# Cluster attention, experts and a bilinear layer: one engine for the low parts of the experts' weights

## The chip, the cores and the metric

One core of a Trainium2 chip runs the kernel. Its engines are TensorE (PE; PEld is its loading of weights), VectorE (DVE), ScalarE (ACT), GpSimd (POOL) and SyncE (SP), which issues most of the DMAs; GpSimd issues the indirect ones. Each works through its own queue in order and waits on semaphores for the others. The metric is the time on the device in microseconds.

## The reference

```python
# attention: 2 x 8 heads, 768 rows of 64; a query sees the keys of its own cluster of 16
q_assign = np.argmax(np.einsum('bhsd,hcd->bhsc', q_n, c_n), axis=-1)
k_assign = np.argmax(np.einsum('bhsd,hcd->bhsc', k_n, c_n), axis=-1)
mask = q_assign[:, :, :, None] == k_assign[:, :, None, :]
scores = np.where(mask, scale * np.matmul(q, k.transpose(0, 1, 3, 2)), -1000000000.0)
x = softmax(scores) @ v                       # then laid out as 1536 tokens x 512
# experts: 8, one to a token, 512 -> 1024 -> 512, times the gate
logits = x @ w_gate
expert_idx = np.argmax(logits, axis=1)
for e in range(E):
    h = np.maximum(x[expert_idx == e] @ w1[e], 0.0)
    out[expert_idx == e] = gate_w[expert_idx == e, None] * (h @ w2[e])
# bilinear layer: 512 -> 1536, weights in float64
return (out @ w_a) * (out @ w_b) @ w_out
```

## The kernel before

The kernel has three stages on the time line of the profile: attention to about 295 us, the experts to 520, the bilinear layer from 526 to the end. Every engine's order is the order in which the program writes its instructions; nothing is scheduled afterwards.

A float32 operand is multiplied as two float32r parts, a high part (`hi`, `xh`, `hh`) that a copy rounds, and a low part (`lo`, `xl`, `hl`) that a subtraction makes from the operand and its high part; a product takes three matmuls. The experts' weights come in pieces of 128 x 1024 elements, 512 KB each, eight to an expert: four of `w1`, then four of `w2`. `piece_load` issues a piece's DMA on SyncE into one of four buffers `raw`, `piece_parts` (lines 129 to 141) makes `hi` on ScalarE and `lo` on the engine that `ENG` names, by the piece's number modulo the length of that list: even pieces on GpSimd, odd ones on VectorE. The load of a piece is issued behind the parts of the piece four before it, and takes its buffer. Pieces 0 and 1 are split during the attention; 35 even and 35 odd ones of the experts follow.

The experts' stage works on windows of 256 tokens, one to an expert, in the order 0 to 3, a spill window of 128 rows (`spill`) for the largest expert, then 4 to 7. In a window (`window`, lines 959 to 988) eight groups of 12 matmuls make the blocks of the hidden layer into three banks in turn; ScalarE makes `hh`, VectorE `hl` from each, so the fourth group needs the bank that the first `hl` frees. Eight more groups make `y`. While they run, the next window's rows are transposed and split (`xh`, `xl`, line 957). At the end `store` copies `y` to `yt`, half on ScalarE, half on VectorE (lines 991, 992).

Side work is spread by `tick`, which each group calls once. It asks for pieces ahead of their use (at tick t up to number `t // 2 + min(LEAD + t // 4, 10)`), and takes one step of the generator `tables`: counts and offsets of the experts, the table of further windows, then `gates` (the softmax's value at the chosen expert, squared) and the places `pu` to which each token's number and gate are scattered (`aux`, by GpSimd; read back behind the loop for further windows, line 1201). `tables` gets a step in each of the first ticks, from tick 1 to 14, and after that in the second half of each window.

```python
    ENG = [("act", "pool"), ("act", "dve")]
    ENG64 = [("act", "pool")]
        if t >= 1 and (t < 15 or t % 16 >= 8):
            next(tab_steps, 0)
```

The weights of the bilinear layer (`ENG64`) are first put from float64 to float32 on VectorE, and their low parts are made by GpSimd.

Of the kernel before, what the change touches and what calls it, by code (L numbers as in the profile page):

```python
# [8 lines left out]
F32 = mybir.dt.float32  # L9
# [20 lines left out]
def cluster_attention__then__moe__then__bilinear_kernel(  # L30
# [37 lines left out]
    # ---- weights in chunks of [128, 1024], each split into two float32r parts  # L68
# [7 lines left out]
    # A piece is what one staging tile holds: a chunk of w1 (256 columns) or of  # L76
    # w2 (256 rows), or half a chunk of w_a, w_b or w_out, which come as float64
    # and are read as pairs of 32-bit words.
# [26 lines left out]
    def piece_bits(n):  # L105
        """First part of a split: float64 to float32."""
        t = raw_t.pop(n)
        i, j = pieces[n]
        if j == 0:
            s = i % NSLOT  # L110
            pn = pools["a" if s < NA else "b"]
            hi_t[i] = pn.tile([128, CH], F32R, tag=f"hi{s}", name=f"hi_{i}")
            lo_t[i] = pn.tile([128, CH], F32R, tag=f"lo{s}", name=f"lo_{i}")
        if i >= MOE2:
            # float64 to float32: sign and top exponent bit stay, the other three
            # bits by which the exponents differ go, the fraction is cut to 23 bits
            # (exact for zeros, and to 24 bits in float32's normal range)
            r = t.rearrange("p (f w) -> p f w", w=2)
            tmp = pools["b"].tile([128, CH // 2], U32, tag="tmp", name=f"tmp_{n}", bufs=2)
            nc.vector.tensor_scalar(out=tmp, in0=r[:, :, 1], scalar1=5, scalar2=2,  # L120
                                    op0=ALU.logical_shift_left, op1=ALU.logical_shift_right)
            nc.vector.scalar_tensor_tensor(out=tmp, in0=r[:, :, 1], scalar=0xC0000000, in1=tmp,  # L122
                                           op0=ALU.bitwise_and, op1=ALU.bitwise_or)
            nc.vector.scalar_tensor_tensor(out=tmp, in0=r[:, :, 0], scalar=29, in1=tmp,  # L124
                                           op0=ALU.logical_shift_right, op1=ALU.bitwise_or)
            t = tmp
        bits_t[n] = t.bitcast(F32)

    def piece_parts(n, hi_eng, lo_eng):
        """Second part of a split: high and low float32r."""  # L130
        raw = bits_t.pop(n)
        i, j = pieces[n]
        hi, lo = hi_t[i], lo_t[i]
        if i >= MOE2:
            hi, lo = (x[:, CH // 2 * j:CH // 2 * j + CH // 2] for x in (hi, lo))
        if hi_eng == "act":
            nc.scalar.copy(out=hi, in_=raw)  # L137
        else:
            nc.vector.tensor_copy(hi, raw)
        eng = nc.gpsimd if lo_eng == "pool" else nc.vector  # L140
        eng.tensor_tensor(out=lo, in0=raw, in1=hi.bitcast(F32), op=ALU.subtract)  # L141
# [5 lines left out]
    # ---- scratch in DRAM: a region of S*B rows for each expert  # L147
# [4 lines left out]
    # ---- constants of the routing  # L152
# [39 lines left out]
    # =========================== attention ===========================  # L192
    # Tiles that are free first come first: the first chunks of the experts' weights
    # take their place before the attention has ended.
# [9 lines left out]
    lg = {}  # L204
# [58 lines left out]
    # Operand stacks of 128 rows, two sets that take turns. First head of a pair:  # L263
    # queries [high; low] and [high; cluster], keys [high; high] and [low; penalty];
    # second head: the halves swapped. The cluster and penalty rows are 16 in 32.
# [8 lines left out]
    # centroids over their norms, laid out as a block diagonal for each head pair  # L274
# [31 lines left out]
    # The norm of a query or key row scales its similarities by one positive  # L306
    # factor, so it does not change which centroid has the largest one.
    class Prep:
        """The steps that lay out the operands of a pair of heads."""
# [17 lines left out]
        def sims(self, tag="X", bufs=1):  # L327
            # similarities, transposed: row 32 g + 16 h + c
            x = ps.tile([128, 512], F32, tag=tag, name=f"sm{self.p}", bufs=bufs)
            for g in range(4):  # L330
                nc.tensor.matmul(
                    x[32 * g:32 * g + 32, 0:GN], lhsT=cblk[:, self.hp, :],
                    rhs=self.raw["qk"[g // 2]][:, GN * (g % 2):GN * (g % 2) + GN], start=True, stop=True,
                )
            self.sim = ap.tile([128, GN], F32, tag="sim", name=f"sim{self.p}")
            nc.scalar.copy(out=self.sim, in_=x[:, 0:GN])
# [21 lines left out]
        def rows(self, nm, tag="X", bufs=1, copies=(act_copy, dve_copy, act_copy, dve_copy)):  # L358
            # cluster rows of the queries, penalty rows of the keys
# [21 lines left out]
        def high(self, nm, h, i, other, copy):  # L381
            """High parts: those of head h, in stack i, own half or (keys) the other one."""
            r = slice(64 * h, 64 * h + 64)
            o = slice(64 - 64 * h, 128 - 64 * h) if other else r
            dst = (qs if nm == "q" else ks)[self.s, h]
            copy(dst[o, i, :], self.raw[nm][r])
# [59 lines left out]
    def pv_steps(p, g, j0=0, nj=NG, tags=("O", "X"), per=1):  # L446
        """Values times probabilities for nj query tiles of a group, in steps."""
# [22 lines left out]
    def emit_x(p, t0, nj, ot, sm, tag):  # L470
        b, hp = pairs[p]
        if hp == 0 and t0 == 0:
            xb[b] = xpool.tile([128, NT, DM], F32, name=f"x{b}")
            lg[b] = xpool.tile([128, NT, E], F32, name=f"lg{b}")
# [21 lines left out]
    # =========================== routing ===========================  # L496
# [4 lines left out]
    def apart(group, inst, why):  # L501
        """Scatters of a group go to rows of their own: none waits for another."""
        inst = inst.ins
        tc.declare_no_dep(inst, group=group, reason=why)
        tc.add_to_no_dep_group(group, inst)
# [7 lines left out]
    def route(b, t0, n, tag="X", place=None):  # L513
        """Experts of n tiles of tokens and the rows of xs that they go to, in steps.
        With place, no scatter, but one-hot rows for the places in the first window."""
# [57 lines left out]
    def gates(b):  # L573
# [8 lines left out]
        nc.vector.tensor_scalar(out=g, in0=g, scalar1=1e-9, scalar2=None, op0=ALU.add)  # L582
        nc.vector.reciprocal(out=g, in_=g)
# [5 lines left out]
    def tables(rps):  # L589
        """Counts and offsets of the experts, positions of the tokens, windows  # L590
        beyond the first, in steps."""
# [15 lines left out]
        # the expert with the most tokens, and where its further window starts  # L607
# [21 lines left out]
        # all windows beyond the first, one to a partition  # L629
# [28 lines left out]
        # start of each window inside its expert, then the three columns of the table  # L658
# [16 lines left out]
        # where the tokens go: number and squared gate of each  # L675
        yield from gates(B - 1)
        dl = cp.tile([128, E], F32, name="dl")
        nc.vector.tensor_tensor(out=dl, in0=off, in1=erow, op=ALU.subtract)
        for b in range(B):
# [3 lines left out]
            nc.vector.tensor_reduce(out=ps_, in_=t, axis=AX.X, op=ALU.add)  # L683
            nc.vector.tensor_tensor(out=ps_, in0=ps_, in1=slot[b], op=ALU.add)
# [9 lines left out]
    # ---- the attention's schedule  # L694
    NU = 12
    LAG = 2
    def keep_warm(n, tag, shape, bufs, pool=ps):
        """The PE array's clock halves when it idles for a few microseconds."""
# [67 lines left out]
    for p in range(1, len(pairs)):  # L766
        for o, step in STEPS:
            if p == 1:
                # no values to multiply yet: the first four steps in two iterations
# [12 lines left out]
    def steps_at(i, gen, n=1, every=1):  # L782
        """The next n steps of gen, one in each of the coming iterations."""
# [13 lines left out]
    # The last group of the last pair goes one query tile after another. The tokens  # L797
    # of its last NP tiles come into the first window by products with one-hot rows,
    # the others by way of xs, where rows not yet written hold zeros.
# [11 lines left out]
    def place_split(t, c0, c1, copy):  # L811
        """Columns of tile t in two float32r parts."""
# [11 lines left out]
    def place_mm(t, d):  # L824
        """Adds the tokens of tile t to the transposed rows of the first window."""
# [75 lines left out]
    # =========================== experts ===========================  # L901
# [11 lines left out]
    def advance(n, engines, later=0):  # L913
        """Splits up to piece n, of the last ones only the first part, and loads."""
# [31 lines left out]
    def win_xt(w, n, a):  # L946
        """Transposes of the rows 128 a ... of a window, and their split."""
# [48 lines left out]
    def spill(w, c0, tick, nxt):  # L996
        """A window of 128 rows with the rows stationary; returns its last part."""
# [68 lines left out]
    ENG = [("act", "pool"), ("act", "dve")]  # L1066
# [29 lines left out]
    # the first banks are those that the first window's rows are read from until late  # L1096
# [56 lines left out]
    # ---- any further windows, one at a time  # L1153
# [42 lines left out]
    # =========================== bilinear layer ===========================  # L1196
# [28 lines left out]
    for gr in range(NGR):  # L1225
        for st in range(NST):
# [3 lines left out]
            for fl in range(GF + 1):  # L1230
# [24 lines left out]
                # of the very last tile of tokens, two blocks together at the end  # L1255
# [49 lines left out]
```

## Time and profile before

| | us |
|---|---|
| median of 3 timed runs | 832.33 |
| lowest and highest | 831.39, 832.38 |
| span of the profiled execution, first to last instruction | 830.4 |
| busy: PE, DVE, ACT, POOL | 793.5, 541.5, 367.1, 292.9 |

The profile gives the execution's own time as its span; what a timed run has beyond that is the little work around it. Busy time is added up over stages with different limits, so what a change in one stage is worth is read from the waits of that stage.

### The profile page before, as it was taken

How to read it: one execution, taken by the hardware profiler on the slowest of the kernel's cores; microseconds unless marked ns; L12 is line 12 of the kernel's file. 1: busy time of each engine (PE TensorE's matmuls, PEld its weight loads, DVE VectorE, ACT ScalarE, POOL GpSimd, SP SyncE). 2: the span in 40 equal slices, each digit the busy share in tenths (PEclk: the TensorE clock that was granted, in tenths of full speed). 3: DMA queues.
4: the chain of work that ended last, by engine and by line, in shares of the span. 5: the costliest groups of instructions: out<-in, count | busy, mean ns of one | idle time of the engine just before them, and what ended most of it. 6: DMA issues, size and time to landing. Idle time of an engine off the chain costs nothing. (4 is left out here: it accounts for less than half of the span.)

```text
span 830.4 us, 12569 instructions
## 1 busy us (share of the span) xinstructions
PE 793.5 (96%) x4832; PEld 639.1 (77%) x4832; DVE 541.5 (65%) x900; ACT 367.1 (44%) x693; POOL 292.9 (35%) x233
## 2 busy tenths in 40 slices
PE   8999999999999988899999999799999999999996
PEld 5666666665666778899999999588888888888885
DVE  6868879778786789555554459874565667624333
ACT  5867667766676454445564542222322212201100
POOL 4915434344540454576553334321121121101011
PEclk9999999999999999799999999899999999999998
DMA  9405012221100155768785654431131120001011
GB/s 299 97 1 159 1 39 63 64 58 45 52 20 1 50 197 167 225 148 221 230 276 184 218 183 153 117 114 51 51 93 60 51 70 32 1 0 51 1 51 51
DMA packets 69949, 81.91 MB, mean 99 GB/s; under 512 B 27264, under 2 KB 48256, under 8 KB 69888
## 3 DMA queue, kind: packets, MB, share of 16 engines
q1 hardware_dynamic: 67584, 74.78, 30.5%
q0 software_dynamic: 2304, 6.31, 2.0%
q8 instruction: 39, 0.64, 0.3%
q14 instruction: 22, 0.18, 0.1%
HBM read 70.58 MB, written 10.50 MB: 98 GB/s over the span
## 5 line engine op out<-in xcount | busy, mean ns | idle before, releaser
L141 POOL TENSOR_TENSOR lo<-raw,hi 128x1024 fp32r<-128x1024 f32 x37 | 92.7, 2509 | 88.8 <-ACT hi L137 43.6
L1242 PE MATMUL ab<-yh,hi 128*128 128x512 f32 x288 | 113.4, 394 | 6.0 <-ACT yh L1214 6.0
L141 POOL TENSOR_TENSOR lo<-tmp,hi 128x512 fp32r<-128x512 f32 x36 | 51.5, 1430 | 179.1 <-ACT hi L137 177.1
L1242 PE MATMUL ab<-yh,lo 128*128 128x512 f32 x288 | 113.1, 393 | 0.0
L1249 DVE TENSOR_TENSOR ga<-ga,ab 128x512 f32<-128x512 f32 x36 | 24.7, 685 | 127.3 <-PE ab L1242 104.4
L417 DVE TENSOR_REDUCE nm<-s 128x1 f32<-128x768 f32 x96 | 91.5, 953 | 17.9 <-PE s L415 12.4
L424 ACT ACTIVATE pr<-s,nm 128x768 f32<-128x768 f32 x96 | 87.2, 908 | 17.6 <-DVE nm L417 16.5
L438 PEld LDWEIGHTS t<-ident,pr 128*128 128x128 f32 x576 | 62.9, 140 | 40.6 <-ACT pr L424 16.8
L415 PE MATMUL s<-ks,qs 128*128 128x512 f32 (+1 forms) x384 | 91.2, 359 | 1.1 <-ACT pr L424 0.6
L438 PE MATMUL t<-ident,pr 128*128 128x128 f32 x576 | 83.8, 279 | 2.8 <-DVE pt L444 2.8
L1248 ACT COPY ga<-ab 128x512 f32<-128x512 f32 x36 | 21.1, 587 | 143.3 <-PE ab L1242 143.3
L453 PE MATMUL o<-pt,vn 128*64 128x384 f32 (+1 forms) x432 | 82.5, 472 | 0.0
L968 PE MATMUL h<-xh,hi 128*128 128x256 f32 x256 | 68.3, 297 | 10.2 <-DVE hl L973 10.0
L137 ACT CAST hi<-raw 128x1024 fp32r<-128x1024 f32 x70 | 72.4, 1047 | 12.6 <-DMA raw<-in_moe_w 12.5
L1242 PE MATMUL ab<-yl,hi 128*128 128x512 f32 x288 | 77.8, 392 | 0.0
L983 PE MATMUL y<-hh,hi 128*128 128x256 f32 x256 | 73.5, 287 | 0.0
L141 DVE TENSOR_TENSOR lo<-raw,hi 128x1024 fp32r<-128x1024 f32 x35 | 61.0, 1746 | 18.0 <-ACT hi L137 17.5
L983 PE MATMUL y<-hh,lo 128*128 128x256 f32 x256 | 72.4, 283 | 0.0
L983 PE MATMUL y<-hl,hi 128*128 128x256 f32 x256 | 72.4, 283 | 0.0
L442 ACT COPY pt<-t 128x384 f32<-128x384 f32 x98 | 46.9, 480 | 54.4 <-PE t L438 52.7
L1242 PEld LDWEIGHTS ab<-yh,hi 128*128 128x128 f32 x288 | 54.8, 190 | 17.6 <-ACT yh L1214 6.2
L415 PEld LDWEIGHTS s<-ks,qs 128*128 128x128 f32 x384 | 58.2, 189 | 12.1 <-issue 3.8
(309 smaller groups left out, 1682.3 us busy)
## 6 DMA issues: line engine op xcount, KB each, us to landing
raw<-in_moe_w SPq DMA_DIRECT2D x72, 512.0 KB, 4.6
raw<-in_moe_w_a SPq DMA_DIRECT2D x12, 512.0 KB, 3.7
raw<-in_moe_w_b SPq DMA_DIRECT2D x12, 512.0 KB, 3.7
raw<-in_moe_w_out SPq DMA_DIRECT2D x12, 512.0 KB, 3.3
xs<-zero SPq DMA_DIRECT2D x8, 512.0 KB, 5.2
xw<-xs SPq DMA_DIRECT2D x15, 256.0 KB, 5.5
vn<-in_v SPq DMA_DIRECT2D x8, 384.0 KB, 3.2
qn<-in_q SPq DMA_DIRECT2D x14, 192.0 KB, 4.8
```

The lines of the kernel that those rows point to most:

```text
L137: nc.scalar.copy(out=hi, in_=raw)
L141: eng.tensor_tensor(out=lo, in0=raw, in1=hi.bitcast(F32), op=ALU.subtract)
L415: nc.tensor.matmul(sc[:, c0:c1], lhsT=w, rhs=ks[s, h][:, i, c0:c1], start=(i == 0), stop=(i == 1))
L417: nc.vector.tensor_reduce(out=nm, in_=sc[:, 0:S], axis=AX.X, op=ALU.max, negate=True)
L424: nc.scalar.activation(out=pr, in_=sc[:, 0:S], func=AF.Exp, bias=nm, scale=1.0, accum_out=sums[p][:, t, h:h + 1])
L438: nc.tensor.transpose(x[:, 128 * n:128 * n + 128], pr[:, 128 * kb:128 * kb + 128], ident)
L442: nc.scalar.copy(out=dst, in_=src)
L453: nc.tensor.matmul(o[64 * h:64 * h + 64, 0:n], lhsT=vn[:, h, kb, :], rhs=pt_t[p, g, h][:, kb, 128 * j0:128 * j0 + n], start=(kb == 0), sto ...
L968: nc.tensor.matmul(hp_[:, 0:n], lhsT=a_[:, d, f0:f0 + 128], rhs=b_[:, d, 0:n], start=(i == 0), stop=(i == len(seq) - 1))
L983: nc.tensor.matmul(y[:, d, 0:n], lhsT=a_[:, fb % 2, 128 * d:128 * d + 128], rhs=b_[:, 0:n], start=(fb == 0 and d % 2 == 0 and i == 0), sto ...
L1242: nc.tensor.matmul(p_, lhsT=a_[:, d, f0:f0 + 128], rhs=b_[d], start=(i == 0), stop=(i == len(seq) - 1))
L1249: nc.vector.tensor_tensor(out=ga, in0=ga, in1=ab[1], op=ALU.mult)
```

## The change

All low parts of the experts' weights are made by VectorE. The logits `lg` are allocated in the pool of constants, which lives to the end, and not with the attention's output. The last batch's `gates` gets one step more, and in `tables` the places get steps of their own: one after `dl`, one after the first sum of each batch.

```diff
-            lg[b] = xpool.tile([128, NT, E], F32, name=f"lg{b}")
+            lg[b] = cp.tile([128, NT, E], F32, name=f"lg{b}")
...
-    def gates(b):
+    def gates(b, fine=False):
...
         nc.vector.tensor_scalar(out=g, in0=g, scalar1=1e-9, scalar2=None, op0=ALU.add)
+        if fine:
+            yield
         nc.vector.reciprocal(out=g, in_=g)
         nc.vector.tensor_tensor(out=auxt[b].bitcast(F32)[:, :, 1], in0=g, in1=g, op=ALU.mult)
         yield
...
-        yield from gates(B - 1)
+
+        yield from gates(B - 1, True)
         dl = cp.tile([128, E], F32, name="dl")
         nc.vector.tensor_tensor(out=dl, in0=off, in1=erow, op=ALU.subtract)
+        yield
         for b in range(B):
...
             nc.vector.tensor_reduce(out=ps_, in_=t, axis=AX.X, op=ALU.add)
+            yield
             nc.vector.tensor_tensor(out=ps_, in0=ps_, in1=slot[b], op=ALU.add)
...
-    ENG = [("act", "pool"), ("act", "dve")]
+    ENG = [("act", "dve")]
```

Comments are taken out too, and lines behind `gates` move down by up to four.

VectorE at the start of the experts' stage, from the last operation of the routing to the last of the first four low parts (the number behind a name is the buffer's; the lines' difference, before with -, after with +):

```order
 L560 TENSOR_TENSOR run_3347<-run_3299,ohe_143 128x8
-L1091 TENSOR_TENSOR xl_3395<-x0t_3301,xh_3394 128x512
-L1091 TENSOR_TENSOR xl_3395<-x0t_3302,xh_3394 128x512
+L141 TENSOR_TENSOR lo_3389<-raw_1068,hi_3388 128x1024
+L1095 TENSOR_TENSOR xl_3395<-x0t_3301,xh_3394 128x512
+L1095 TENSOR_TENSOR xl_3395<-x0t_3302,xh_3394 128x512
 L141 TENSOR_TENSOR lo_3401<-raw_1070,hi_3400 128x1024
+L141 TENSOR_TENSOR lo_3407<-raw_1366,hi_3406 128x1024
 L141 TENSOR_TENSOR lo_3413<-raw_1736,hi_3412 128x1024
```

Four low parts in place of two stand ahead of the first window's `hl`, the first of them ahead of the window's `xl`.

VectorE from the end of the gates to the second `hl` of the second window, before:

```order
L584 TENSOR_TENSOR auxt_84<-gg_3788 128x6
L141 TENSOR_TENSOR lo_3794<-raw_3654,hi_3793 128x1024
L678 TENSOR_TENSOR dl<-offs,erow 128x8
L681 TENSOR_TENSOR pt_3813<-ohe_142,dl 128x48
L683 TENSOR_REDUCE ps_3815<-pt_3813 128x6
L684 TENSOR_TENSOR ps_3815<-ps_3815,slot_144 128x6
L686 CAST pu_3818<-ps_3815 128x6
L992 ISA
L992 COPY yt<-y_3426 128x2x256
L973 SCALAR_TENSOR_TENSOR hl_0_3855<-h_0_3841,hh_0_3854 128x256
L141 TENSOR_TENSOR lo_3865<-raw_3751,hi_3864 128x1024
L973 SCALAR_TENSOR_TENSOR hl_1_3884<-h_1_3870,hh_1_3883 128x256
```

The same place now, from the sum of the gates on:

```order
L582 TENSOR_SCALAR gg_3788<-gg_3788 128x6
L141 TENSOR_TENSOR lo_3792<-raw_3654,hi_3791 128x1024
L585 RECIPROCAL gg_3788<-gg_3788 128x6
L586 TENSOR_TENSOR auxt_84<-gg_3788 128x6
L996 ISA
L996 COPY yt<-y_3426 128x2x256
L977 SCALAR_TENSOR_TENSOR hl_0_3843<-h_0_3829,hh_0_3842 128x256
L141 TENSOR_TENSOR lo_3847<-raw_3701,hi_3846 128x1024
L141 TENSOR_TENSOR lo_3853<-raw_3751,hi_3852 128x1024
L977 SCALAR_TENSOR_TENSOR hl_1_3872<-h_1_3858,hh_1_3871 128x256
```

The five operations from `dl` to `pu` have left the place ahead of the first `hl` (they follow in the window's second half), the last two of the gates stand behind the low part and not ahead of it, and a second low part stands ahead of the second `hl`. GpSimd's queue, which held 35 low parts between and behind its scatters there, holds the twelve scatters of `aux` alone until the bilinear layer's weights.

## Rows read from the trace of the kernel before

**Rows 1.** Busy time: length, PE, PEld, DVE, ACT, POOL, PEclk, DMA share, GB/s.

```profile
303.40:307.40 4.00, 4.00 (x21) 4.00 (x22) 3.72 (x14) 0.38 (x1) 2.17 (x1) 0.57 0.75 259
...
335.00:345.00 10.00, 9.21 (x43) 8.92 (x44) 5.71 (x7) 4.13 (x8) 5.56 (x2) 0.53 0.87 246
...
430.00:450.00 20.00, 20.00 (x170) 20.00 (x169) 9.41 (x13) 10.64 (x17) 7.76 (x4) 1.00 0.74 244
```

**Rows 2.** Timeline, TensorE's waits: start, length, instruction, [idle before <-releaser].

```profile
303.40 0.58 PE L968 MATMUL h<-xh,hi 128*128 128x256 f32 x1 [2.91 <-DVE hl L973]
...
327.78 0.74 PE L968 MATMUL h<-xl,hi 128*128 128x256 f32 x4 [2.09 <-DVE xl L957]
...
335.03 0.58 PE L968 MATMUL h<-xh,hi 128*128 128x256 f32 x1 [3.63 <-DVE hl L973]
...
338.72 0.58 PE L968 MATMUL h<-xh,hi 128*128 128x256 f32 x1 [0.76 <-DVE hl L973]
...
366.35 0.38 PE L968 MATMUL h<-xh,hi 128*128 128x256 f32 x1 [1.01 <-DVE hl L973]
...
415.13 0.50 PE L1032 MATMUL y<-hi,sl 128*128 128x512 f32 x1 [0.48 <-DVE sl L1023]
```

**Rows 3.** Timeline of VectorE, long rows of the experts' stage.

```profile
296.91 4.97 DVE L141 TENSOR_TENSOR lo<-raw,hi 128x1024 fp32r<-128x1024 f32 x1
...
304.00 1.60 DVE L604 CAST offi<-offs 128x8 int32<-128x8 f32 x1
...
310.99 2.00 DVE L639 TENSOR_TENSOR wcum<-wcum,wnw 128x1 f32<-128x1 f32 x1
...
315.76 2.04 DVE L639 TENSOR_TENSOR wcum<-wcum,wnw 128x1 f32<-128x1 f32 x1
...
318.21 2.21 DVE L645 TENSOR_TENSOR wn<-wn 128x1 f32<-128x1 f32 x1
...
323.35 2.17 DVE L666 TENSOR_TENSOR wst<-wva,ecol 128x80 f32<-128x80 f32 x1
...
362.43 3.54 DVE L141 TENSOR_TENSOR lo<-raw,hi 128x1024 fp32r<-128x1024 f32 x1 [0.51 <-ACT hi L137]
```

**Rows 4.** Timeline of GpSimd beside them.

```profile
296.02 4.76 POOL L141 TENSOR_TENSOR lo<-raw,hi 128x1024 fp32r<-128x1024 f32 x2
...
318.01 2.40 POOL L141 TENSOR_TENSOR lo<-raw,hi 128x1024 fp32r<-128x1024 f32 x1 [0.23 <-ACT hi L137]
```

**Rows 5.** Low parts by tile (min/median/max ns), and VectorE's group of the page.

```profile
L141 POOL TENSOR_TENSOR lo<-raw,hi x37: 2367/2406/3387, 119.3 to 487.2; 128x1024 fp32r<-128x1024 f32 x37
...
L141 DVE TENSOR_TENSOR lo<-raw,hi x35: 1209/1226/4967, 296.9 to 490.5; 128x1024 fp32r<-128x1024 f32 x35
...
L141 DVE TENSOR_TENSOR lo<-raw,hi 128x1024 fp32r<-128x1024 f32 x35 | 61.0, 1746 | 18.0 <-ACT hi L137 17.5
```

**Rows 6.** Timeline of VectorE, stage's start and second window's first `hl`.

```profile
295.48 1.29 DVE L1091 TENSOR_TENSOR xl<-x0t,xh 128x512 fp32r<-128x512 f32 x2 [2.16 <-ACT xh L1089]
...
332.50 0.16 DVE L678 TENSOR_TENSOR dl<-offs,erow 128x8 f32<-128x8 f32 x1
...
333.37 0.17 DVE L686 CAST pu<-ps 128x6 uint32<-128x6 f32 x1
...
334.56 0.41 DVE L973 SCALAR_TENSOR_TENSOR hl<-h,hh 128x256 fp32r<-128x256 f32 x1
```

**Rows 7.** Timeline of ScalarE, the gates' exponential and the next high part.

```profile
330.15 0.24 ACT L578 ACTIVATE gl<-gl 128x48 f32<-128x48 f32 x1 [7.21 <-DVE gl L577]
...
330.30 1.03 ACT L137 CAST hi<-raw 128x1024 fp32r<-128x1024 f32 x1
```

**Rows 8.** Timeline of GpSimd, scatters of places alone and beside a low part.

```profile
361.46 0.97 POOL L688 DMA_INDIRECT aux<-auxt,pu  x1 [0.30 <-issue]
...
365.04 1.80 POOL L688 DMA_INDIRECT aux<-auxt,pu  x1 [0.16 <-PE h L968]
```

**Rows 9.** Waits: who waited for whom, us in total, times, longest.

```profile
ACT hi L137 <- DMA raw<-in_moe_w: 12.5, 11, 1.9
```

## Prediction

> **What bounds the kernel now.** I read the table of stages first. In a window of the experts' stage that has got going, TensorE is busy all the time: 170 matmuls in 20.00 us at clock 1.00, so 0.118 us for one [rows 1]. There no change on another engine can give anything. What the change can give or take is therefore where TensorE waits in that stage, and for that I listed TensorE's waits from 300 to 420 us in order of time [rows 2]. The reader is to see what released each of them. All six end with a VectorE instruction: `hl` (the low part of a hidden block), `xl` (the low part of a window's rows) or `sl` (the same for the spill). They are 2.91, 2.09, 3.63, 0.76, 1.01 and 0.48 us. After two of the six the clock falls to its lower level: a granted clock of 0.57 over 4 us is 4 x 0.43 / 0.5 = 3.4 us at 1.2 GHz, and 0.53 over 10 us is 9.4 us of it [rows 1]. Each such microsecond costs half of itself.
>
> Next, why VectorE is late there. Seven of its rows are far too long for what they do [rows 3]: an addition of one element per partition takes 2.00 and 2.04 us. Put beside GpSimd's rows [rows 4] they end together: 318.21 + 2.21 = 320.42 against GpSimd's 318.01 + 2.40 = 320.41. The low part at 296.91 ends at 301.88, which is 1.10 us after GpSimd's two ended at 300.78: it did its own work only then. So a VectorE instruction between operands in SBUF stands still until GpSimd's low part is through. The table by tile says the same: VectorE's low parts have a median of 1.226 us and a maximum of 4.967 us [rows 5].
>
> **The change part by part.** From piece 2 on, 35 low parts go from GpSimd to VectorE. Up to the first `hl` of the second window, seven of them move.
>
> *What goes away.* With nothing but the places' scatters left on GpSimd, the six long rows of the first window shrink to their own length: 4.97 - 1.23 = 3.7, and 1.60 + 2.00 + 2.04 + 2.21 + 2.17 less five times 0.2 (a small operation, [rows 6], takes 0.16 or 0.17, a few of these some more) = 9.0. Together 12.7 us.
>
> *What is added.* The first of the seven falls into VectorE's 2.16 us of idle time ahead of the first `xl` [rows 6]; it costs nothing as long as that cover stands, and 1.2 us without it. The other six cost 6 x 1.23 = 7.4 us.
>
> *What is moved out.* The five small operations from `dl` to `pu`, 332.50 to 333.54 = 1.0 us [rows 6], stood between the last low part and the first `hl` of the second window; now they come in that window's second half, where TensorE doesn't wait for VectorE.
>
> *A wait that is laid bare.* ScalarE makes the high part of piece 15 behind the gates' exponential, 0.24 + 1.03 us [rows 7]. VectorE now comes to that piece's low part only some 0.4 us after the exponential and stands about 0.8 us. Behind it in its queue are the copy of `y` and the first `hl`.
>
> Sum to the first `hl` of the second window: 12.7 + 1.0 - 7.4 - 0.8 = 5.5 us earlier. It ended at 334.56 + 0.41 = 334.97 [rows 6], so now at 329.5, and TensorE's fourth group of that window starts then and not at 335.03. The fifth group needs the next `hl`, with two low parts ahead of it in the new order: 329.5 + 2 x 1.23 + 0.42 = 332.4 against 338.72 [rows 2], which is 6.3 us earlier.
>
> The first two waits can't be added to that. The first shrinks to about half a microsecond: low parts 3, 4 and 5 end at 296.9 + 3 x 1.23 = 300.6, `hl` at 301.0, TensorE is there at 303.40 - 2.91 = 300.5. That gives 2.4, the 3.4 us of low clock behind it give 1.7, the second wait 2.1: TensorE is 6.2 us earlier at its fourth group, ready at 335.03 - 3.63 - 6.2 = 325.2, and waits there until 329.5. So the longest wait stays, at 4.3 us; the whole ramp is now set by VectorE's queue. After a wait of that length I expect the clock to fall again, as it did after 2.91 and 3.63 us. Of the 9.4 us at the low level before, some 5.7 lay behind 338.72 and cost 2.8. Now the level may last between 3.4 and 9.4 us from 329.5 on, so 0.5 to 6.5 us behind 332.4, at a cost of 0.3 to 3.2. I take the middle, 1.7, since nothing in the rows says which of the two it resembles: a gain of 1.1, between -0.4 and 2.5.
>
> *Later windows.* The wait of 1.01 us at 366.35 follows a low part of 3.54 us that GpSimd held up; at 1.23 it is 2.3 us earlier, and the wait goes. The spill's 0.48 goes in the same way. Together 1.5. New waits should not come: in two groups (24 matmuls, 2.8 us) VectorE has one low part and two `hl`, 1.23 + 2 x 0.42 = 2.1 us, and three banks of hidden blocks leave an `hl` two groups, 2.8 us, less 0.4 on ScalarE (an estimate, from `hl`) and 0.4 of its own: 2.0 us of room for a low part of 1.23. A load of weights waits for the low part four pieces back; those come sooner.
>
> *At nothing.* The logits' place moves no instruction, only addresses, and no row has a price for that; I take nothing, since every engine's order is otherwise that of the other edits. The twelve scatters of places come a window later; they are read behind the loop after 526 us, more than 100 us on.
>
> In all 6.3 + 1.1 + 1.5 = 8.9 us. The profiled execution shows a span of 830.4, the median of the timed runs is 832.33, so about 1.9 lies around it, unchanged: 832.3 - 8.9 = 823.4 us.
>
> *A rule weighed.* The rows say that VectorE stands until GpSimd's instruction ends. The Trainium skill, SBUF — State Buffer, section SBUF: two separate sides, calls the port pair that the two engines share an exclusive lock, held for a whole instruction by the one that starts first, not a split of bandwidth. Against this change the same section warns that a VectorE instruction which holds the pair keeps GpSimd from writing the descriptors of its DMAs. By the first the low parts run at 1.23 and the sum is as above; by the second the scatters are held. The trace shows that too: a scatter beside a low part took 1.80 us, one alone 0.97 [rows 8]. What it does here is the fourth rival.
>
> **The rivals.**
> *VectorE's low parts cost more than 1.23 when all are there.* Before, their mean was 61.0 / 35 = 1.74 us [rows 5]. Were that their own price, six more would cost 10.4 and the seven that stood there would give nothing back of their excess: 12.7 - 3.7 + 1.0 - 10.4 - 0.8 = -1.2, and with the 1.5 of the later windows no change, 832. Against it: the median of 1.226 [rows 5], and that the long ones end with GpSimd's.
> *The ramp's wait goes too.* If VectorE's small operations close up more than I count, or the clock stays up, the gain is 8.9 + 2 to 4, and at most all six waits, 10.9 us, with the low clock's 1.7 + 4.7 = 6.4: 17.3 us, 815. The sum of VectorE's work speaks against it.
> *Slower: high parts that wait for weights now hold up `hl`.* Half of the low parts used to wait on GpSimd, where nobody stood behind them. Now every one stands in VectorE's queue ahead of an `hl`, and waits for a high part, which waits for its load. From 2.0 us on such a wait reaches TensorE. Before, ScalarE waited 11 times for weights, 12.5 us in all, at most 1.9 [rows 9]. Were each a microsecond longer on VectorE's side and in the half of a window that counts, 11 x 1 = 11 us would come on, two more than the gain: 834.5. It decides from about 0.95 us each on. Against it: ScalarE's `hh` stood behind the same waits before, and TensorE did not wait for it.
> *Scatters held by VectorE.* Three scatters of token rows end at 296 with a low part beside them; at 0.83 more each they are 2.5 us late, which only matters if the second window's rows are late by more than the some 7 us until their transposes. It would give 0; if not, up to 2.5 off the gain, 826.
>
> **How the numbers follow.** Forecast (7 to 12 us gained): 0.60. Ramp's wait gone or the clock up (over 12): 0.10. A smaller gain, from a longer low clock, dearer low parts or held scatters (2 to 7): 0.17. No change: 0.07. Slower: 0.06. About 0.2% (1.7 us) is what a measurement of this kernel can tell from no change. So faster 0.87, same 0.07, slower 0.06. The range reaches from the upper bound of the gain less its last part, 816.5, to the smaller gains, 829.5; beyond it are 0.05 and 0.14.
>
> **What would show it.** No VectorE row over 1.5 us between 296 and 490 but those that wait for a high part; GpSimd empty there but for scatters; TensorE's waits at 303 and 327 under 0.7 us; one wait of 3.5 to 5 us in the second window's fourth group, near 329, with a low clock behind it; none at 366; from 370 to the end all rows alike and 8 to 10 us earlier. Wrong if low parts stay at 1.7 us with GpSimd idle, or if TensorE waits for `hl` in several later windows.

## The result and the profile after

The changed kernel takes 821.66 us (median of four runs, 819.09 to 823.80), the kernel before 832.36 in the runs beside it: a ratio of 0.9848, with a 95% interval from 0.9816 to 0.9879. That is 10.7 us less where 8.9 were forecast, and inside the range. The profiled execution of the changed kernel has a span of 822.0 us and took 823.78.

TensorE's timeline shows where the experts' stage begins and ends. In the kernel before (start, length, instruction, idle time before it and what ended it):

```profile
295.49 0.39 PE L968 MATMUL h<-xh,hi 128*128 128x256 f32 x1 [0.26 <-ACT xh L1089]
...
526.30 0.80 PE L1242 MATMUL ab<-yh,hi 128*128 128x512 f32 x1 [6.01 <-ACT yh L1214]
```

And in the kernel after, with its waits, which answer to [rows 2]:

```profile
300.01 0.38 PE L972 MATMUL h<-xh,hi 128*128 128x256 f32 x1 [0.26 <-ACT xh L1093]
...
305.31 0.39 PE L972 MATMUL h<-xh,hi 128*128 128x256 f32 x1 [0.31 <-DVE hl L977]
...
331.97 0.39 PE L972 MATMUL h<-xh,hi 128*128 128x256 f32 x1 [2.50 <-DVE hl L977]
...
334.58 0.39 PE L972 MATMUL h<-xh,hi 128*128 128x256 f32 x1 [0.91 <-DVE hl L977]
...
410.54 0.63 PE L957 MATMUL xt<-ident,xw 128*128 128x128 f32 x4 [0.32 <-issue]
...
494.60 0.39 PE L972 MATMUL h<-xh,hi 128*128 128x256 f32 x1 [1.36 <-DVE hl L977]
...
517.63 0.80 PE L1246 MATMUL ab<-yh,hi 128*128 128x512 f32 x1 [5.94 <-ACT yh L1218]
```

From the first `h` matmul to the first of the bilinear layer it is 526.30 - 295.49 = 230.81 us before and 517.63 - 300.01 = 217.62 after: 13.2 us less. The attention ahead of it took 4.5 us longer in this execution, and lost that time in its first 21 us; the same kernel run again did not (last section). So the stage is measured from its own start below.

Of the six waits, those at 327.78, 366.35 and 415.13 are gone, the first is 0.31, the long one 2.50 and the one behind it 0.91 us; one of 0.32 in the spill is new. Added up, the waits from 300 to 420 us fall from 10.88 to 4.04 us, 6.8 less. The windows of the kernel after, in the columns of [rows 1]:

```profile
302.00:306.00 4.00, 3.69 (x36) 3.45 (x35) 3.89 (x10) 2.80 (x6) 0.00 (x0) 1.00 0.96 319
328.00:332.00 4.00, 1.50 (x14) 1.30 (x12) 2.97 (x8) 3.94 (x8) 0.00 (x0) 1.00 0.90 263
332.00:336.00 4.00, 3.09 (x24) 2.88 (x24) 4.00 (x6) 1.66 (x4) 0.00 (x0) 1.00 1.02 347
336.00:346.00 10.00, 10.00 (x86) 10.00 (x85) 7.22 (x15) 5.88 (x9) 0.18 (x1) 1.00 0.76 247
```

The granted clock is 1.00 behind both waits, where [rows 1] had 0.57 and 0.53. The 3.4 and 9.4 us at the lower level that the prediction reads from those rows cost about half of themselves, some 6 us, so nearly half of the stage's gain is the clock's and the rest is waiting. VectorE's timeline in the same stretch (answers to [rows 3, 6]):

```profile
297.75 1.22 DVE L141 TENSOR_TENSOR lo<-raw,hi 128x1024 fp32r<-128x1024 f32 x1
299.99 1.29 DVE L1095 TENSOR_TENSOR xl<-x0t,xh 128x512 fp32r<-128x512 f32 x2 [1.03 <-ACT xh L1093]
301.43 3.50 DVE L141 TENSOR_TENSOR lo<-raw,hi 128x1024 fp32r<-128x1024 f32 x3
...
329.02 1.23 DVE L141 TENSOR_TENSOR lo<-raw,hi 128x1024 fp32r<-128x1024 f32 x1 [0.53 <-ACT hi L137]
...
331.51 0.41 DVE L977 SCALAR_TENSOR_TENSOR hl<-h,hh 128x256 fp32r<-128x256 f32 x1
331.84 2.35 DVE L141 TENSOR_TENSOR lo<-raw,hi 128x1024 fp32r<-128x1024 f32 x2
```

The low parts by tile (min/median/max ns; answer to [rows 5]):

```profile
L141 DVE TENSOR_TENSOR lo<-raw,hi x70: 1212/1225/1228, 297.7 to 481.9; 128x1024 fp32r<-128x1024 f32 x70
```

All 70 lie within 16 ns, where 35 of them reached up to 4967 ns.

### The profile page after: what moved, and what is told of

Same layout as the page of the kernel before. It is cut to its first block, busy times and chain, and to the rows that moved or that the text cites. A ratio compares the mean times of both kernels' runs of the same rounds, so it can differ in the third digit from the quotient of the medians.

```text
span 822.0 us, 12542 instructions
## 1 busy us (share of the span) xinstructions
PE 792.3 (96%) x4832; PEld 635.7 (77%) x4832; DVE 553.2 (67%) x935; ACT 366.8 (45%) x693; POOL 205.8 (25%) x198
## 5 line engine op out<-in xcount | busy, mean ns | idle before, releaser
L141 DVE TENSOR_TENSOR lo<-raw,hi 128x1024 fp32r<-128x1024 f32 x70 | 84.6, 1223 | 19.3 <-ACT hi L137 18.2
L972 PE MATMUL h<-xh,hi 128*128 128x256 f32 x256 | 64.9, 286 | 5.6 <-DVE hl L977 5.4
L444 DVE COPY pt<-t 128x384 f32<-128x384 f32 x94 | 51.6, 549 | 20.9 <-PE t L438 19.9
```

Source lines behind the costliest of these rows:

```text
L444: nc.vector.tensor_copy(dst, src)
L972: nc.tensor.matmul(hp_[:, 0:n], lhsT=a_[:, d, f0:f0 + 128], rhs=b_[:, d, 0:n], start=(i == 0), stop=(i == len(seq) - 1))
```

## The experiments

One table for all; the text takes them one by one. The times are medians of all executions; stage and stretch are those of the one profiled execution of each kernel. "Stage" is from the first `h` matmul to the first `ab` matmul, "stretch" from the first `xl` of the first window to the end of the second window's first `hl` (for the kernel after 331.51 + 0.41 - 299.99 = 31.9). The kernel before took 835.07 us (median) beside the first four, 836.31 beside the next four and 835.93 beside the last two.

| kernel | us, median | ratio to before | stage | stretch |
|---|---|---|---|---|
| before | 832.36 | | 230.81 | 39.5 |
| after | 821.66 | 0.985 | 217.62 | 31.9 |
| low parts alone | 822.82 | 0.984 (0.979 to 0.989) | 218.29 | 32.6 |
| steps alone | 833.65 | 0.997 (0.995 to 1.000) | 226.99 | 38.7 |
| after, GpSimd busy for nothing | 837.28 | 1.003 (1.001 to 1.006) | 233.08 | 40.4 |
| all low parts on GpSimd | 848.59 | 1.014 (1.009 to 1.019) | 244.62 | 44.8 |
| after, again | 822.21 | 0.984 (0.981 to 0.988) | 217.61 | 31.9 |
| after, late low parts too | 821.67 | 0.983 (0.980 to 0.986) | 218.78 | 31.9 |
| after, slower lead | 820.43 | 0.982 (0.979 to 0.985) | 215.98 | 29.8 |
| both | 820.73 | 0.981 (0.978 to 0.984) | 217.83 | 29.8 |
| after, wait of 4.2 | 824.95 | 0.986 (0.983 to 0.990) | 220.17 | 33.7 |
| after, wait of 6.7 | 828.27 | 0.991 (0.988 to 0.994) | 223.13 | 36.2 |

**Low parts alone.**

```diff
 (before)
-    ENG = [("act", "pool"), ("act", "dve")]
+    ENG = [("act", "dve")]
```

> The kernel before with one part of the change alone: every low part of the experts' weights from piece 2 on goes to VectorE; gates, places and logits stay as before. Measure beside the time: from the start of the first xl of the first window to the end of the first hl of the second window, 39.5 us before and 31.9 us after. Theory (GpSimd's low parts make VectorE stand still): nearly the whole gain, less the 1.0 us from dl to pu that stands ahead of that hl again: 32.9 us, and 822.7 us (821 to 824.5). Rival (the smaller steps bring the gain): 38 to 39.5 us, and 830 to 832 us.

Measured: stretch 32.6 (32.9 expected), 822.82 us. The low parts alone bring nearly the whole gain. TensorE's wait is longer than in the kernel after, by 0.66 us:

```profile
331.03 0.39 PE L968 MATMUL h<-xh,hi 128*128 128x256 f32 x1 [3.16 <-DVE hl L973]
```

Behind it the clock stays up as well (columns as in [rows 1]):

```profile
332.00:336.00 4.00, 3.09 (x26) 2.89 (x25) 3.53 (x7) 1.19 (x4) 3.27 (x3) 1.00 0.82 154
```

**Steps alone.**

```diff
 (after)
-    ENG = [("act", "dve")]
+    ENG = [("act", "pool"), ("act", "dve")]
```

> The other part alone: smaller steps of gates and places and the logits in the pool of constants, with every second low part on GpSimd as before. Theory: VectorE's long rows stay; 1.0 us (dl to pu) leaves the stretch, so 38.5 us from the first xl to the first hl of the second window, and 831.3 us (829.5 to 832.5). Rival: 32 to 33 us, and 821 to 823 us.

Measured: stretch 38.7, and 833.65 us, 1.4 less than the kernel before beside it. The steps alone are worth 39.5 - 38.7 = 0.8 us in the stretch, the low parts alone 39.5 - 32.6 = 6.9; together 7.7, and the whole change has 7.6. In the stretch the two parts add up, and the rival falls. In the stage they don't: the steps alone give 230.81 - 226.99 = 3.8 us, the low parts 12.5, the whole change 13.2. Nearly all of the 3.8 is the clock of this execution, for TensorE's waits add up to 10.6 us where the kernel before has 10.9. Behind its wait of 2.90 us it stays at 1.00 (309 to 313 us), where the kernel before fell behind 2.91, and behind 3.49 us it is back at 1.00 after 3.4 us (0.66 from 333.65 to 337.65), where the kernel before took 9.4. The time gives no more than 1.4 us, with an interval that reaches to no change. The logits' place, which is in this run too, costs nothing that shows.

**GpSimd busy for nothing.** Beside every second piece GpSimd subtracts a high part from itself; no result depends on it.

```diff
 (after, in piece_parts)
+        if n > NA and i < MOE2 and i % 2 == 0:
+            idle = pools["b"].tile([128, CH], F32, tag="idle", name=f"idle_{n}", bufs=1)
+            nc.gpsimd.tensor_tensor(out=idle, in0=hi.bitcast(F32), in1=hi.bitcast(F32), op=ALU.subtract)
```

> The kernel after, and beside it for every second piece one GpSimd subtraction of a low part's size (128x1024), hi minus hi, into a tile of its own that nobody reads. Nobody waits for it; VectorE's instructions are those of the kernel after. Theory (one engine stands while the other's instruction between operands in SBUF runs): VectorE's long rows come back on top of its seven more low parts; 12.7 us of stalls before, so 38 to 44 us from the first xl to the first hl of the second window, rows of VectorE above 2 us that end with GpSimd's, and 832 to 838 us. Rival (it only matters who makes the low parts and behind whom they queue; both engines run side by side): 31.9 us, no row of VectorE above 1.5 us, and 819 to 824 us as after.

Measured: stretch 40.4, 837.28 us, 15.1 us more than the kernel after. VectorE's timeline:

```profile
305.42 0.81 DVE L609 CAST offi<-offs 128x8 int32<-128x8 f32 x1
...
314.44 0.41 DVE L980 SCALAR_TENSOR_TENSOR hl<-h,hh 128x256 fp32r<-128x256 f32 x1
314.77 1.93 DVE L644 TENSOR_TENSOR wcum<-wcum,wnw 128x1 f32<-128x1 f32 x3
```

GpSimd's beside it:

```profile
304.31 1.90 POOL L144 TENSOR_TENSOR idle<-hi 128x1024 f32<-128x1024 f32 x1 [2.10 <-ACT hi L137]
...
314.40 1.90 POOL L144 TENSOR_TENSOR idle<-hi 128x1024 f32<-128x1024 f32 x1 [2.10 <-ACT hi L137]
```

The cast ends at 306.23, GpSimd's instruction at 306.21. The three additions end at 316.70, 0.40 behind GpSimd's 316.30; three of them take 0.54 us where GpSimd is idle (316.95 in the same timeline). The `hl` at 314.44, which reads `h` from PSUM, runs beside the same instruction in its usual 0.41 us. Nobody waits for these GpSimd instructions, and VectorE's own list is that of the kernel after: the standing still makes the loss, the longer waits of TensorE behind it and the clock that falls behind two of them included:

```profile
338.27 0.58 PE L975 MATMUL h<-xh,hi 128*128 128x256 f32 x1 [2.55 <-DVE hl L980]
```

```profile
338.00:342.00 4.00, 3.30 (x13) 3.00 (x14) 4.00 (x6) 2.78 (x5) 2.49 (x2) 0.50 0.89 294
```

The other is a wait of 4.98 us that ends at 330.60 (clock 0.60 from 330 to 334). The Trainium skill, SBUF — State Buffer, section SBUF: two separate sides, says that the engine that starts first holds the shared ports for a whole instruction; the ends of these rows agree.

**All low parts on GpSimd.**

```diff
 (after)
-    ENG = [("act", "dve")]
+    ENG = [("act", "pool")]
```

> The kernel after with all low parts from piece 2 on on GpSimd, none on VectorE. Theory: GpSimd makes one in 2.4 to 2.5 us and VectorE stands for most of that; 14 low parts up to the second window's first hl are 34 us on GpSimd alone, so that stretch gets 42 to 48 us, and TensorE waits for VectorE and for low parts: 838 to 850 us, slower than before. Rival without standing still: VectorE is rid of 14 x 1.23 = 17 us in the stretch, only GpSimd's own 34 us count, 34 to 36 us, and 824 to 828 us.

Measured: stretch 44.8, 848.59 us, as the theory had it. VectorE's timeline:

```profile
303.04 12.21 DVE L606 CAST offi<-offs 128x8 int32<-128x8 f32 x1
```

GpSimd's:

```profile
298.89 16.33 POOL L141 TENSOR_TENSOR lo<-raw,hi 128x1024 fp32r<-128x1024 f32 x7
```

A cast of 8 numbers per partition ends at 315.25, GpSimd's seven low parts at 315.22: VectorE did not get its turn between them. TensorE's waits:

```profile
315.63 0.58 PE L972 MATMUL h<-xh,hi 128*128 128x256 f32 x1 [9.39 <-DVE hl L977]
...
412.85 1.12 PE L957 MATMUL xt<-ident,xw 128*128 128x128 f32 x4 [6.33 <-DMA xw<-xs]
```

The second is new in kind. A window's rows are issued by SP behind weight loads, as SP's queue shows; the loads of a weight wait for the buffer of the piece four back, which a low part frees:

```profile
377.18 26.13 SPq L101 DMA_DIRECT2D raw<-in_moe_w  x8
403.51 0.35 SPq L948 DMA_DIRECT2D xw<-xs  x1
```

**After, again**, with nothing edited, as the measure for the next three.

> The kernel after, unchanged, as the measure for the next three on the same chip, and for what differs between executions: it took 819.1 and 819.5 us in two and 823.8 in two. The profile of a 823.8 has the transposes of the first queries and keys at 0.42 and 0.69 us each until 15.8 us, the kernel before has them at 0.30 and 0.43 from 6.45 us on. If that is what parts the two groups, profiles with the slow rows up to 15.8 us are 4 to 4.6 us longer than those without, and nothing else of that size differs. If not, the slow rows and the time do not go together.

Measured: 822.21 us (five of 821.77 to 822.78, one of 827.23). Its stage is 217.61 us, the first profile's 217.62. What parts the executions is told in the last section.

**Late low parts too.**

```diff
 (after)
-    ENG64 = [("act", "pool")]
+    ENG64 = [("act", "dve")]
```

> The kernel after, with the low parts of the bilinear layer's weights (72 halves of 128x512) on VectorE too. Theory: there GpSimd's low part of 1.4 us holds one of the three tmp operations of each half up, 1.67 instead of 0.69; VectorE's own low part costs 0.6 to 0.7 and the stall of 0.98 goes, so VectorE gets no busier, no tmp row is above 1 us, TensorE's waits of 1.36 and 0.29 us near 495 us go: 1.5 us less than the kernel after (0.5 to 2). Rival: 72 more instructions on VectorE outweigh the stalls; the waits near 495 us grow to 2 us and more, and it is 0.5 to 3 us slower than the kernel after.

Measured: 821.67, 0.5 us less than the kernel after beside it. The theory is half right. VectorE's timeline shows no held operation any more, each `tmp` row is 0.42 or 0.69:

```profile
487.93 0.42 DVE L120 TENSOR_SCALAR tmp<-raw 128x512 uint32<-128x512 uint32 x1
488.38 0.69 DVE L122 SCALAR_TENSOR_TENSOR tmp<-raw,tmp 128x512 uint32<-128x512 uint32 x1
489.11 0.69 DVE L124 SCALAR_TENSOR_TENSOR tmp<-raw,tmp 128x512 uint32<-128x512 uint32 x1
...
490.49 0.69 DVE L141 TENSOR_TENSOR lo<-tmp,hi 128x512 fp32r<-128x512 f32 x1 [0.35 <-ACT hi L137]
491.10 0.42 DVE L120 TENSOR_SCALAR tmp<-raw 128x512 uint32<-128x512 uint32 x1
```

But from one half's first `tmp` operation to the next it is 491.10 - 487.93 = 3.17 us, and it was 3.10 in the kernel after (488.28 to 491.38): the own low part and a wait of 0.35 for its high part take the place of the stall. TensorE's wait near 495 is 1.25 and not 1.36, the 0.29 behind it is gone, and the first `ab` matmul waits 6.68 and not 6.07. The stage is 1.2 us longer, what lies behind it 820.3 - 516.87 = 303.4 us, 1.0 shorter. Of the 1.2, 0.9 is not from the edit's place at all: at 409.38 us, in the spill, TensorE stands 1.09 us with no releaser that the trace names, where the kernel after beside it stood 0.21. In sum almost nothing.

**Slower lead.**

```diff
 (after, in tick)
-        n = t // 2 + min(LEAD + t // 4, NSLOT - 2)
+        n = t // 2 + min(LEAD + t // 8, NSLOT - 2)
```

> The kernel after, with the lead of the weights growing by one piece in 8 steps of the schedule, not in 4: up to the second window's first hl VectorE makes two low parts fewer. Theory (VectorE's queue alone sets TensorE's wait of 2.50 us there): 2 x 1.15 = 2.3 us less from the first xl to that hl, 29.6 instead of 31.9; the wait shrinks to 0.2 to 0.5 us and the 0.91 behind it to 0.3 or nothing: 2.5 to 3.2 us less than the kernel after. Rival: with fewer pieces ahead the weights come too late; ScalarE's waits for weights and VectorE's for high parts grow, TensorE waits in the first three windows for low parts or hl, and the time is the same or up to 5 us longer.

Measured: stretch 29.8 (29.6 expected), 820.43 us, 1.8 less than the kernel after, where 2.5 to 3.2 were expected. TensorE's waits:

```profile
331.32 0.39 PE L972 MATMUL h<-xh,hi 128*128 128x256 f32 x1 [0.34 <-DVE hl L977]
...
333.92 0.39 PE L972 MATMUL h<-xh,hi 128*128 128x256 f32 x1 [0.90 <-DVE hl L977]
...
382.38 0.39 PE L972 MATMUL h<-xh,hi 128*128 128x256 f32 x1 [0.33 <-DVE hl L977]
```

The wait of 2.48 becomes 0.34, as the stretch gets 2.15 us shorter: VectorE's queue set it. The 0.90 behind it stays, since its two low parts ahead of the next `hl` stay; and one of 0.33 is new. This is the lowest median of the kernels run, 0.3 us below that of both edits, which is less than one kernel's executions differ by.

**Both.**

> Both edits, the late low parts on VectorE and the slower growth of the lead: they touch waits in different windows, so the sum, 4 to 4.7 us less than the kernel after, and below both kernels of this study. If the two rivals hold, 0 to 8 us more.

Measured: 820.73 us, no better than the slower lead alone. The stage is 1.9 us longer than with the lead alone, 1.1 of it in the wait of the first `ab` matmul (7.16 for 6.06); what lies behind the stage is 0.7 shorter. The sum that was expected does not come: the slower lead gives its 1.8, the late low parts nothing.

**A longer wait.** VectorE gets two subtractions more ahead of the second window's first `hl`.

```diff
 (after, in gates)
         if fine:
+            more = hi_t[nparts[0] - 1].bitcast(F32)
+            idle = pools["b"].tile([128, CH], F32, tag="idle", name="idle", bufs=1)
+            for c in (CH, CH):
+                nc.vector.tensor_tensor(out=idle[:, 0:c], in0=more[:, 0:c], in1=more[:, 0:c], op=ALU.subtract)
             yield
```

> The kernel after, with two more VectorE subtractions of 128x1024 ahead of the reciprocal, into a tile that nobody reads: 2 x 1.15 less the 0.53 us that VectorE idles there anyway = 1.8 us, so TensorE's wait in the second window's fourth group is 4.3 us and not 2.5, the wait that the prediction counted on. Theory of the prediction (a wait of that length brings the clock to its lower level): granted clock of 0.5 to 0.9 in the windows behind the wait, 1.8 us for the wait and another 1.5 to 3 for the low clock: 3.3 to 4.8 us more than the kernel after from the first h matmul to the first of the bilinear layer (217.6). Rival (the wait alone does not do it, the waits of the kernel before before it counted too): clock 1.00 throughout, 1.8 us more.

Measured: TensorE's timeline, and the window behind the wait (columns as in [rows 1]):

```profile
332.45 0.58 PE L976 MATMUL h<-xh,hi 128*128 128x256 f32 x1 [4.24 <-DVE hl L981]
```

```profile
328.00:332.00 4.00, 0.21 (x2) 0.01 (x1) 3.58 (x7) 3.91 (x7) 0.00 (x0) 1.00 0.50 171
332.00:336.00 4.00, 3.55 (x17) 3.55 (x17) 4.00 (x7) 0.41 (x2) 0.00 (x0) 0.57 1.00 311
336.00:340.00 4.00, 4.00 (x36) 4.00 (x35) 2.65 (x5) 1.70 (x3) 0.00 (x0) 1.00 0.92 341
```

The clock falls for 4 x 0.43 / 0.5 = 3.4 us and costs 1.7. The stage grows by 2.6 us, less than the 3.3 to 4.8 expected: 1.75 for the wait and 1.7 for the clock, less the wait of 0.91 behind it, which the slower matmuls cover.

**The same with four** (`for c in (CH, CH, CH, CH)`).

> The same with four such subtractions: 4 x 1.15 - 0.53 = 4.1 us, a wait of 6.6 us. If the clock falls behind the 4.3 us of the run before, it falls here too, and the low clock's extra over the longer wait says whether its price grows with the wait: 5.6 to 7.1 us more than the kernel after in that stage. If it fell there not, this tells whether a wait alone can do it: clock below 0.9 behind the wait, or 4.1 us and 1.00 throughout.

Measured: a wait of 6.74 us, the stage 5.5 longer. The windows behind it:

```profile
332.00:336.00 4.00, 1.01 (x4) 1.02 (x5) 3.62 (x8) 0.00 (x0) 0.00 (x0) 0.58 0.33 99
336.00:340.00 4.00, 4.00 (x22) 4.00 (x22) 3.33 (x6) 0.38 (x1) 0.00 (x0) 0.56 0.98 340
340.00:344.00 4.00, 4.00 (x35) 4.00 (x35) 2.41 (x4) 2.60 (x5) 0.00 (x0) 1.00 0.63 221
```

Of 5.5, 6.74 - 2.50 = 4.24 are the longer wait, and the wait of 0.91 is covered as before, so the low clock cost 5.5 - 4.24 + 0.91 = 2.2 us, against 1.7 in the run before: not much more.

## Why the prediction was right, and where it was off

*The mechanism holds.* GpSimd's low parts made VectorE stand; without them VectorE's low parts take 1.22 us, and with a GpSimd instruction of no use the loss comes back. That the low parts are dear of themselves is refuted by the 70 rows.

*The stretch to the second window's first `hl`: 7.6 us earlier, 5.5 predicted.* This term was too small. The six added low parts cost 7.0 and not 7.4: 1.23 is what one takes alone, and those that stand in a row overlap a little (3.50 for three). The operations moved out gave 0.7 (32.6 against 31.9) and not 1.0. The wait laid bare was 0.53 and not 0.8. The rest is in the stalls: VectorE was busy 36.32 us of that stretch before and 29.05 after, 7.27 less; with 7.0 added and 0.7 moved out, the stalls come to 13.6 by difference, not to the 12.7 that the long rows alone gave. VectorE's idle time fell by 0.3 and did not grow by 0.8.

*The fifth group: 8.7 us earlier, 6.3 predicted* (338.72 - 295.49 = 43.23, and 334.58 - 300.01 = 34.57). It follows from the step before.

*TensorE's readiness was right, its wait not.* TensorE was to be ready 325.2 - 295.48 = 29.7 us behind the first `xl`; it was ready after 331.97 - 2.50 - 299.99 = 29.5. Since `hl` came 2.1 us sooner than predicted, the wait was 2.50 and not 4.3.

*The low clock: the step that failed.* It was to come back and leave a gain of 1.1; it did not come back. In the kernel before it cost, behind the fifth group (length, TensorE busy, PEclk, DMA share, GB/s):

```profile
338.72:342.00 3.28, 3.28 (x15) 0.50 0.77 94
342.00:346.00 4.00, 4.00 (x27) 0.70 0.93 326
```

3.28 x 0.50 + 4.00 x 0.30 = 2.8 us, all of which the change gives back. In the run with a wait of 4.24 us, nearly the one predicted, the clock does fall, for 3.4 us. So the term failed because the wait that it hung on was sized at 4.3 and measured 2.50. That a wait of 2.50 us leaves the clock up is shown for this kernel and is no rule: with 2.91 us it fell in the kernel before and with 2.55 where GpSimd was busy for nothing, with 3.16 it stayed up in the low parts alone. What else decides stays open.

*Later windows* gave the 1.01 and the 0.48 us, as predicted; in the spill 0.32 stand in their place, released by nothing that the trace names. ScalarE's waits for weights sank:

```profile
ACT hi L137 <- DMA raw<-in_moe_w: 6.7, 10, 2.1
```

They were 12.5 us [rows 9], so the rival of held high parts does not come up. Of the scatters of token rows one, which started at 298.25 beside a low part, took 1.56 us, the others 0.97 to 1.04, and it held up nothing: the wait for the second window's `xl` is gone.

So the stage gives 8.7 + 2.8 + 1.5 - 0.3 = 12.7 us (the last for the new wait in the spill), against 13.2 measured and 8.9 forecast; 0.5 us is not accounted for. By its mechanism that is the second rival, *The ramp's wait goes too*, at 0.10: VectorE's operations closed up more than was counted, and the clock stayed up.

*That the time came out near the forecast is luck.* Two executions of the kernel after took 819.09 and 819.54 us, 13 less than the kernel before; two took 823.78 and 823.80 and pull the median to a gain of 10.7. The profiled one of these began 4.5 us late; the other has no profile. In the later runs the two kernels took 836.31 and 822.21 us, 14.1 apart.

## What to carry to other kernels

Rows of VectorE that are too long for their size and end with a GpSimd row are a price of the GpSimd work, however little anyone waits for that: ask what VectorE would need for it itself. Here six low parts, 7.0 us in all, took the place of 13.6 us of stalls. Where such a move shortens a wait of TensorE, work out the time for both cases, with the clock falling behind the new wait and with the clock staying up (2.8 us apart here behind the fifth group), for the wait's length did not tell which it would be. And look at the queue ahead of the wait: two low parts fewer took 2.1 of the 2.5 us that were left.

## What the runs showed of the hardware that was not expected

*Two starts.* In the profile of the kernel before the first transposes get shorter from 6.45 us on:

```profile
5.83 0.69 PE L322 MATMUL xq<-ident,qn 128*64 128x128 f32 x2
6.45 0.30 PE L321 MATMUL xq<-ident,qn 128*64 128x128 f32 x1
6.68 0.43 PE L322 MATMUL xq<-ident,qn 128*64 128x128 f32 x2
```

That of the kernel after, with the same instructions, has them long to the last:

```profile
15.46 0.42 PE L321 MATMUL xk<-ident,kn 128*64 128x128 f32 x1
15.81 0.69 PE L322 MATMUL xk<-ident,kn 128*64 128x128 f32 x2
```

The windows print a granted clock of 1.00 for both stretches, but no reading stands behind that: the trace's first clock entry begins at 6.45 us in the kernel before, where the rows get shorter, and at 20.63 us in the kernel after. Four of the twelve profiles have the long rows: after, steps alone, slower lead, both. In these four the first entry (full clock) begins at 17.53 to 20.66 us, in the other eight at 4.45 to 6.55. So the late starts are those in which TensorE gets its full clock late; that it ran at the lower level until then is inferred from the rows, and why it rises late in some executions stays open: from 1.36 us on TensorE worked without a gap in both kernels, up to these places.

In time the long rows go with 4.2 us (after: 823.78, its other three executions with a median of 819.54), 3.4 (slower lead: 823.66 against 820.22) and 5.7 (both: 826.44 against 820.51), but with no more than 0.8 in the run with the steps alone (834.30 against 833.52, in a kernel whose times spread over 6 us). In the second profile of the kernel after the rows are short, and its time, 821.84, is among the lower ones there. It is still above 819.09: this profile, like nine others, has a wait of 2.2 us of VectorE near 289 us that ends from outside the core's engines ("remote" in the view), and the first profiles of the two kernels do not have it.

*A turn that is not given.* Seven GpSimd instructions in a row kept one VectorE cast waiting for 12.21 us; in the same run, from 321.70 us on, VectorE got in one or two operations behind each. Operations on `h` in PSUM were never held: the 64 `hl` lie between 0.41 and 0.43 us in that run.

*The clock's fall.* Waits of 2.00 (GpSimd busy for nothing, the first), 2.09 (before), 2.50 (after), 2.90 (steps alone, the first) and 3.16 us (low parts alone) left the clock up; 2.55 and 4.98 (GpSimd busy for nothing), 2.91 and 3.63 (before), 3.49 (steps alone, the second), 4.24 and 6.74, and 4.29, 6.33 and 9.39 (all low parts on GpSimd) went with the lower level. Length alone does not tell the two groups apart. In the attention the same place shows both: in all twelve profiles TensorE waits 1.5 us and soon after 0.5 us near 205 to 210 us, and in six of them the clock then falls (0.50 from 205.84 to 209.25 us in the second profile of the kernel after), in the other six, the kernel before among them, it reads 1.00. The six in which it falls are those whose first clock entry begins earliest, at 4.45 to 5.05 us; more than that the runs do not show.
